# Expert phase of an mLSTM + two-MLP kernel: order of four engines written out by hand, six staging places for weights, a place for each slot's token weights

## The chip, the cores and the metric

One core of a Trainium2 chip runs the whole program. The metric is device time in microseconds (us) of one execution; lower is better. Times are medians of repeated runs on the chip; the profile is one further execution, recorded by the hardware profiler.

## What is computed

Three parts follow each other. An mLSTM recurrence (batch 4, 8 heads, 768 steps, head size 40) makes 3072 rows of 320 numbers. A dense MLP (320 to 2048 to 320, `h * sigmoid(h)` between) maps them. Then a top-1 mixture of eight experts follows, and this is the part that the change touches:

```python
logits = x @ w_gate                      # 3072 x 8
expert_idx = np.argmax(logits, axis=1)
...                                      # gate_w: the chosen expert's softmax weight
for e in range(8):
    xe = x[expert_idx == e]
    h = np.maximum(xe @ w1[e], 0.0)      # 320 -> 1024
    out[expert_idx == e] = gate_w[expert_idx == e, None] * (h @ w2[e])
```

## The kernel before

*Phase one* runs the recurrence in six chunks of 128 steps beside the dense MLP of the chunk before. While it runs, `rows(c)` routes each chunk: it finds each token's expert (`experts`), its row within the expert's list in DRAM (`place`), a power-of-two scale (`scale`), the gate weight (`weights`), and, in four `halves`, writes the token's 386-word row (value as a high and a low f16 half, gate weight, token number) to `rows_x` with an indirect store on GpSimd (POOL, line 931).

*Phase two* works through 28 *slots* of 128 tokens of one expert, listed in `line`: three early slots whose rows were fetched during phase one (`fetch_early`), 21 slots at offsets `kofi` that the last routing gives, and four late slots whose expert is known only at run time (`later_slots` computes it). A slot is

- `fetch`: SyncE (SP) reads the offset into a register, issues a transposing DMA of 128 rows into `xT` (line 1197) and a small DMA of gate weight and token number into `xm` (line 1199, pool of 5 buffers);
- `m_l1`: two halves of 32 matmuls of 128x128 (line 1212) into one of two PSUM buffers `ps_l1`; ScalarE (ACT) applies Relu and makes the high half `hh` (line 1217); VectorE (DVE) makes the low half `hl` (line 1218). A PSUM buffer is free when its `hl` is made;
- `m_l2`: 24 matmuls of 128x320 (lines 1231 to 1233); DVE scales into `ym` (line 1235, 2 buffers) and adds up the target row `sid` (line 1242, 3 buffers); POOL stores the 128 rows to the output (line 1243).

The experts' f32 weights come in 4 groups of 704 KB per expert (`load_w`: three or four DMAs on SP, lines 539 to 549) into one of two staging places of the pool `stg`. `go` makes the f16 high halves on ACT (lines 554, 555), its `tail` the low halves on DVE (lines 558, 562, 566), both into `w_all`; then the place is free. Experts 0 to 3 are loaded at fixed points of phase one (`at(p, ...)`, conversion 4 points later). The other 32 groups, experts 4 to 7 and four late experts, which take the room of experts 0 to 3, go through `weights_load` and `weights_split` in the slots' loop: on average 1.5 groups a slot, the next load of a place right after the conversion was recorded.

None of these lines fixes the order in which an engine gets its instructions. The framework's scheduler reorders them by dependences, priorities and a cost model of its own, engine by engine; each engine then runs its list strictly in order, and an instruction that waits holds back all behind it. The weights' conversions (ACT, DVE) and the slots' `hh`, `hl`, `ym`, `sid` share these lists, and the loads and fetches share SP's.

Of the kernel before, what the change touches and what calls it, by code (L numbers as in the profile page):

```python
# [33 lines left out]
def mlstm_moe_kernel(ctx, tc, q, k, v, ig, fg, og, w_in, w_out, w_gate, w1, w2, out):  # L34
# [127 lines left out]
    stg = ctx.enter_context(tc.tile_pool(name="stg", bufs=2))  # L162
# [369 lines left out]
    def load_w(k, g, e):  # L532

        cs = slice(g * GF, (g + 1) * GF)
        ts = stg.tile([128, WI], F32, tag="wi", name="e12")
# [6 lines left out]
        else:  # L542
            ee = bass.ds(e, 1)
            nc.sync.dma_start(out=t[:, 0:2, :], in_=w1[ee, 0:256, cs].rearrange("e (j p) f -> p (e j) f", p=128))
            for r in range(2):
                nc.sync.dma_start(
                    out=t[64 * r:64 * r + 64, 2, :], in_=w1[ee, 256:320, cs].rearrange("e p f -> p (e f)")
                )
# [24 lines left out]
    with contextlib.nullcontext():  # L573
# [446 lines left out]
        xme = const.tile([128, NE, 2], F32, name="xme")  # L1020
        done = const.tile([128, E], F32, name="done")

        def fetch_early():
            for i, (e, n) in enumerate(EARLY):
# [4 lines left out]
                xm[e, n] = xme[:, i, :]  # L1029
# [63 lines left out]
        for cf in todo:  # L1093
            l2(*cf)
        tails = []
        for i in range(2):
            rowt.append(th_v[i][:, 0:RW])
            nc.gpsimd.memset(rowt[-1][:, 352:384], 0.0)
        for fn in rows(NC - 1):
            t = fn()  # L1100
            while tails:
                tails.pop()()
            if callable(t):
                tails.append(t)
        tails.pop()()
# [4 lines left out]
        pn = ps_at.tile([128, E], F32, tag="at", name="ps_n")  # L1110
        nc.tensor.matmul(pn, ones, cum[:, NTT, :], start=True, stop=True)
# [7 lines left out]
        nc.vector.memset(zer, 0.0)  # L1119
        nc.vector.tensor_scalar(out=num, in0=pn, scalar1=-128.0, scalar2=None, op0=ALU.add)  # L1120

# [7 lines left out]
        nc.vector.tensor_tensor(out=kpos, in0=iota_k, in1=done.unsqueeze(2).to_broadcast(sk), op=ALU.add)  # L1129
        nc.vector.tensor_tensor(out=kfit, in0=kpos, in1=num.unsqueeze(2).to_broadcast(sk), op=ALU.min)  # L1130
        nc.vector.tensor_tensor(out=kofi, in0=kfit, in1=ebase.unsqueeze(2).to_broadcast(sk), op=ALU.add)
        nc.vector.tensor_tensor(out=kpos, in0=kpos, in1=kfit, op=ALU.subtract)
        nc.vector.tensor_scalar(out=kneg, in0=kpos, scalar1=iota_p, scalar2=NONE, op0=ALU.is_gt, op1=ALU.mult)
# [56 lines left out]
        hT = {}  # L1190

        def fetch(i, row):
# [8 lines left out]
        def m_l1(i, k):  # L1201
            x = xT.pop(i)
            hh = mp.tile([128, NF2, 128], F16, tag="hh", name="hh")
            hl = mp.tile([128, NF2, 128], F16, tag="hl", name="hl")
            hT[i] = (hh, hl)
            for r in range(2):
                ps = ps_l1.tile([128, 4, 128], F32, tag="l1", name="ps_m1")
                for jj in range(4):
                    f = 4 * r + jj
                    terms = [(0, 0), (1, 1), (2, 2), (3, 0), (4, 1), (0, 3), (1, 4), (2, 5)]  # L1210
                    for n, (a, m) in enumerate(terms):
# [43 lines left out]
        def later(i):  # L1255
            return ((E + i, 0), i % ND, ofi[0:1, i:i + 1], neg[:, i:i + 1])
# [89 lines left out]
```

## Time and profile before

| | us |
|---|---|
| median of 3 runs | 814.64 (805.28 to 817.34) |
| the profiled execution's own time | 814.33 |
| its span in the profile | 812.2 |
| TensorE (PE) busy in the span | 689.3 |
| mean granted TensorE clock, 1.0 = full | 0.925 |

A row of the timeline view reads: start, length, engine, source line, operation, output <- inputs, count, and in brackets how long the engine had sat idle and what released it. SPq is SyncE's queue, where the length is that of issuing the DMA. A row of the waits view reads: who <- for whom: us in total, times, longest. A row of the windows view gives the busy time of each engine in a stretch, and at its end granted clock, share of the 16 DMA engines, and GB/s moved.

### The profile page before, as it was taken

What the parts mean: (1) busy time and instruction counts of PE and PEld (TensorE: products, weight loads), DVE (VectorE), ACT (ScalarE), POOL (GpSimd) and SP (SyncE); (2) the same over time, 40 slices, a digit from 0 to 9 for tenths busy, and PEclk for the clock granted to TensorE, in tenths of its full rate; (3) what the DMA queues carried; (4) which work ended last, traced back from release to release, by engine and by line L of the source; (5) the groups of instructions that cost most, each with busy time, mean ns of one, the idle gap of its engine ahead of it and who ended that gap; (6) DMA issues with size and microseconds to landing.
All of it is one profiled execution on the core that took longest, in us unless ns stands there. A gap on an engine that the chain in (4) does not pass through costs nothing. (4 is left out here: it accounts for less than half of the span.)

```text
span 812.2 us, 15662 instructions
## 1 busy us (share of the span) xinstructions
PE 689.3 (85%) x5840; PEld 490.0 (60%) x5840; DVE 513.3 (63%) x1262; ACT 375.8 (46%) x816; POOL 98.6 (12%) x134
## 2 busy tenths in 40 slices
PE   4866999998888999889998977996685978878994
PEld 3724766765555556556665634555575867767883
DVE  6686689888778856676777566457555355544231
ACT  5563467766566545556654354435233233332110
POOL 3010001112001211020011001101100000111110
PEclk9677799999899999999999998997979998999997
DMA  8757898997889565453441243224675555565210
GB/s 156 145 133 190 199 175 211 211 177 170 167 170 175 117 124 102 89 118 79 93 88 52 72 130 104 50 67 135 143 177 137 100 155 142 144 145 122 52 25 22
DMA packets 243309, 102.83 MB, mean 127 GB/s; under 512 B 181621, under 2 KB 237112, under 8 KB 243224
## 3 DMA queue, kind: packets, MB, share of 16 engines
q1 hardware_dynamic: 239860, 92.99, 53.9%
q0 software_dynamic: 2880, 8.68, 2.9%
q8 instruction: 48, 0.79, 0.4%
q14 instruction: 37, 0.30, 0.1%
q10 hardware_dynamic: 484, 0.08, 0.1%
HBM read 71.64 MB, written 11.59 MB: 102 GB/s over the span
## 5 line engine op out<-in xcount | busy, mean ns | idle before, releaser
L961 PE MATMUL ps_h<-w_all 128*128 128x512 f16 x768 | 194.6, 393 | 10.8 <-ACT w_all L466 5.5
L1212 PEld LDWEIGHTS <-w_all 128*128 128x128 f16 x1792 | 116.7, 106 | 42.0 <-issue 40.2
L1212 PE MATMUL ps_m<-xT,w_all 128*128 128x128 f16 x1600 | 106.5, 233 | 35.0 <-DVE hl L1218 35.0
L961 PEld LDWEIGHTS <-w_all 128*128 128x128 f16 x768 | 74.7, 101 | 87.9 <-issue 15.2
L1005 PE MATMUL ps_y<-w_all 128*128 128x328 f16 x332 | 102.2, 308 | 7.3 <-ACT w_all L1013 6.7
L554 ACT ACTIVATE w_all<-e 128x768 f16<-128x768 f32 x48 | 40.4, 842 | 134.1 <-DMA e<-in_moe_w_dram 124.1
L1007 PE MATMUL ps_y<-w_all 128*128 128x328 f16 x332 | 101.8, 307 | 0.3 <-DVE w_all L988 0.3
L1006 PE MATMUL ps_y<-w_all 128*128 128x328 f16 x332 | 101.9, 307 | 0.0
L988 DVE SCALAR_TENSOR_TENSOR w_all<-w_all 128x512 f16<-128x512 f32 x83 | 57.2, 689 | 39.3 <-ACT w_all L985 38.4
L558 DVE SCALAR_TENSOR_TENSOR w_all<-e,w_all 128x512 f16<-128x512 f32 x48 | 33.1, 689 | 75.4 <-ACT w_all L554 72.7
L985 ACT ACTIVATE w_all<-w_all 128x512 f16<-128x512 f32 x83 | 51.9, 625 | 56.9 <-DVE w_all L980 56.5
L241 ACT ACTIVATE w_all<-w_all,bias_t 128x128 f32<-128x128 f32 x160 | 52.9, 391 | 41.8 <-POOL w_all L207 41.7
L1231 PE MATMUL ps_m<-w_all,hh 128*128 128x320 f16 x224 | 67.2, 300 | 5.8 <-ACT hh L1217 5.8
L1232 PE MATMUL ps_m<-w_all,hh 128*128 128x320 f16 x224 | 67.3, 301 | 0.0
L1233 PE MATMUL ps_m<-w_all,hl 128*128 128x320 f16 x224 | 67.3, 300 | 0.0
L980 DVE SCALAR_TENSOR_TENSOR w_all<-w_all,ps_h 128x512 f32<-128x512 f32 x83 | 56.5, 681 | 14.2 <-ACT w_all L977 14.0
L1217 ACT ACTIVATE hh<-ps_m 128x512 f16<-128x512 f32 x56 | 32.3, 590 | 68.8 <-PE ps_m L1212 65.6
L977 ACT ACTIVATE w_all<-ps_h 128x512 f32<-128x512 f32 x83 | 48.5, 585 | 23.7 <-PE ps_h L961 22.0
L1218 DVE SCALAR_TENSOR_TENSOR hl<-ps_m,hh 128x512 f16<-128x512 f32 x56 | 38.3, 685 | 27.6 <-ACT hh L1217 27.5
L318 PEld LDWEIGHTS ps_pv<-w_all 128*128 128x128 f32 x384 | 50.6, 207 | 7.0 <-issue 2.7
L318 PE MATMUL ps_pv<-w_all 128*128 128x41 f32 x384 | 50.4, 293 | 3.6 <-issue 2.0
L1243 POOL DMA_INDIRECT out_dram<-ym,sid x28 | 27.8, 992 | 206.6 <-DVE ym L1235 187.5
(210 smaller groups left out, 1123.1 us busy)
## 6 DMA issues: line engine op xcount, KB each, us to landing
e<-in_moe_w_dram SPq DMA_DIRECT2D x48, 320.0 KB
e<-in_moe_w_dram SPq DMA_DIRECT2D x48, 256.0 KB
w_all<-lam_d SPq DMA_DIRECT2D x20, 512.0 KB
w_all<-in_moe_w_out_dram SPq DMA_DIRECT2D x16, 320.0 KB
wi<-in_moe_w_in_dram SPq DMA_DIRECT2D x8, 512.0 KB
e<-in_moe_w_dram SPq DMA_DIRECT2D x32, 128.0 KB
w_all<-in_k_dram SPq DMA_DIRECT2D x24, 160.0 KB
w_all<-in_q_dram SPq DMA_DIRECT2D x24, 160.0 KB
```

Source lines behind the costliest of these rows:

```text
L241: nc.scalar.activation(out=lt[:, h, :], in_=lt[:, h, :], func=AF.Exp, bias=bias_t[:, c, b * H + h:b * H + h + 1])
L318: nc.tensor.matmul(pv[:, h, :], u["lam"][:, h, :], u["v"][:, h, :], start=True, stop=True)
L961: nc.tensor.matmul(ps, a, x, start=(i == 0), stop=(i == len(terms) - 1))
L980: nc.vector.scalar_tensor_tensor(out=th, in0=th, scalar=1.0, in1=ps, op0=ALU.add, op1=ALU.mult)
L988: nc.vector.scalar_tensor_tensor(out=gl, in0=th, scalar=SG, in1=gh, op0=ALU.mult, op1=ALU.subtract)
L1005: nc.tensor.matmul(ps, gh[:, ts], woh[:, f, :], start=(f == 0), stop=False)
L1006: nc.tensor.matmul(ps, gh[:, ts], wol[:, f, :], start=False, stop=False)
L1007: nc.tensor.matmul(ps, gl[:, ts], woh[:, f, :], start=False, stop=(f == NF - 1))
L1212: nc.tensor.matmul(ps[:, jj, :], w1c[k][:, a, f * 128:f * 128 + 128], x[:, m, :], start=(n == 0), stop=(n == len(terms) - 1),)
L1231: nc.tensor.matmul(ps, hh[:, f, :], w[:, 0, :], start=(f == 0), stop=False)
L1232: nc.tensor.matmul(ps, hh[:, f, :], w[:, 1, :], start=False, stop=False)
L1233: nc.tensor.matmul(ps, hl[:, f, :], w[:, 0, :], start=False, stop=(f == NF2 - 1))
```

## The change

1. From the last two `l2` calls of phase one to the last slot, everything stands inside `tc.manual_schedule` for PE, ACT, DVE and SP: these four get their instructions in the order of the source. POOL stays with the scheduler.
2. The source is rewritten as a pipeline: `m_l1` is split into `m_half`; the last `rows(NC - 1)` is dealt out between the halves of slots 0 and 1; a slot `i` is: fetch of slot `i + 2`, half 0, low halves of one weight group and the next load into its place, `hl`, half 1, `hl`, one conversion (on odd slots from 7 one more of each), then the second layer of slot `i - 1`.
3. Staging has six places: `stg` has 3 buffers, and from slot 5 on three more (`more`) lie in the room of expert 0, whose slots are over. The late experts therefore use the rooms of experts 1 to 4.
4. `xm` gets a place for each of the 28 slots (`xms`); `xT` rotates over the four buffers `Qs`, `Ks`; `ym` has 4 buffers, `sid` 6.
5. In phase one, the conversion stands 8 (experts 0, 1) or 7 points after the load instead of 4. A run-time expert's third weight part is one DMA instead of two.

```diff
-    stg = ctx.enter_context(tc.tile_pool(name="stg", bufs=2))
+    stg = ctx.enter_context(tc.tile_pool(name="stg", bufs=3))
...
-            at(p + 4, lambda: w_go.pop(0)())
+            at(p + (8 if i < 2 * NG else 7), lambda: w_go.pop(0)())
...
+        xT_b = turns([x[:, 0:6, :] for x in Ks[1:] + Qs + Ks[:1]])
...
-            xT[i] = mp.tile([128, 6, 128], F16, tag="xT", name="xT")
+            xT[i] = next(xT_b)
             nc.sync.dma_start_transpose(out=xT[i], in_=r.bitcast(F16)[:, 0:768])
-            xm[i] = mp.tile([128, 2], F32, tag="xm", name="xm", bufs=5)
+            if i in place_of:
+                xm[i] = xms[:, place_of[i], :]
...
-            y = mp.tile([128, DM], F32, tag="ym", name="ym", bufs=2)
+            y = mp.tile([128, DM], F32, tag="ym", name="ym", bufs=4)
...
-            sid = mp.tile([128, 1], I32, tag="sid", name="sid")
+            sid = mp.tile([128, 1], I32, tag="sid", name="sid", bufs=6)
...
+        more = [F32V[:, i * WI:(i + 1) * WI] for i in range(WN // (2 * WI))]
...
+        def split():
+
+            if w_go:
+                go, place = w_go.pop(0)
+                w_low.append((go(), place))
+
+        def low_and_load():
+
+            if w_low:
+                t, place = w_low.pop(0)
+                t()
+                load(place)
...
+        with tc.manual_schedule(engines={ENG.PE, ENG.Activation, ENG.DVE, ENG.SP}):
+
+            for cf in todo:
+                l2(*cf)
...
+            for i in range(NE, NE + 2):
+                get(i)
+            for i in range(2, len(line)):
+                if i > 2:
+                    get(i + 2)
+                t = half(i, 0)
+                low_and_load()
+                t()
+                if i > 5 and i % 2:
+                    split()
+                t = half(i, 1)
+                t()
+                if i > 5 and i % 2:
+                    low_and_load()
+                if i == 3:
+                    later_slots()
+                split()
+                if i == 5:
+                    for x in more:
+                        load(x)
+                second(i - 1)
+            second(len(line) - 1)
```

ACT at the seam of the phases, before: L1013 evicts the dense MLP's last results (`ps_y`), L554 and L555 convert a weight group (`e_...` is its staging place), L1217 is a slot's Relu.

```order
L554 ACTIVATE w_all<-e_6020 128x3x256
L555 ACTIVATE w_all<-e_6020 128x2x320
L1013 ACTIVATE w_all<-ps_y_5234 128x328
L1013 ACTIVATE w_all<-ps_y_5238 128x328
L1013 ACTIVATE w_all<-ps_y_5242 128x328
L1013 ACTIVATE w_all<-ps_y_5246 128x328
L554 ACTIVATE w_all<-e_6061 128x3x256
L555 ACTIVATE w_all<-e_6061 128x2x320
L1217 ACTIVATE hh<-ps_m_5867 128x512
```

The same place of the changed kernel; its L1011, L1208 and L858 are the L1013, L1217 and L860 of before (L858 is an exponential of the routing).

```order
L1011 ACTIVATE w_all<-ps_y_5234 128x328
L1011 ACTIVATE w_all<-ps_y_5238 128x328
L1011 ACTIVATE w_all<-ps_y_5242 128x328
L1011 ACTIVATE w_all<-ps_y_5246 128x328
L1208 ACTIVATE hh<-ps_m_5796 128x512
L858 ACTIVATE le<-ld 128x32
L1208 ACTIVATE hh<-ps_m_5845 128x512
```

The two conversions ahead of and behind the evictions are gone from here: the first conversion of phase two now stands behind both Relus of slot 2.

SP in the middle of phase two, before: the fetch of a slot (L1197, L1199) and the load of a weight group (L544 to L549).

```order
L1197 DMA_TRANSPOSE xT<-rows_x 128x6x128
L1199 ISA
L1199 DMA xm<-rows_x 128x2
L544 ISA
L544 DMA e_7155<-in_moe_w_dram 128x2x256
L546 ISA
L546 DMA e_7155<-in_moe_w_dram 64x256
L546 ISA
L546 DMA e_7155<-in_moe_w_dram 64x256
L549 ISA
L549 DMA e_7155<-in_moe_w_dram 128x2x320
```

After, slots 7 and 8: two loads (L540 to L542) and the fetch for slot 10 with its register load (L1180 to L1188).

```order
L540 DMA e_6758<-in_moe_w_dram 128x2x256
L541 DMA e_6758<-in_moe_w_dram 128x1x256
L542 DMA e_6758<-in_moe_w_dram 128x2x320
L540 DMA e_6803<-in_moe_w_dram 128x2x256
L541 DMA e_6803<-in_moe_w_dram 128x1x256
L542 DMA e_6803<-in_moe_w_dram 128x2x320
L1180 TENSOR_LOAD kofi
L1180 ISA x2
L1183 ISA
L1183 DMA_TRANSPOSE Ks_109<-rows_x 128x6x128
L1188 ISA
L1188 DMA xms<-rows_x 128x2
```

The `xm` DMA, behind which each load stood before, now writes a place that nothing else uses; what remains ahead of a load is the fetch two slots ahead and the conversion that frees the load's own place.

## Rows read from the trace of the kernel before

**Rows 1.** The page's head.
```profile
span 812.2 us, 15662 instructions
```

**Rows 2.** Windows view of stretches of phase two.
```profile
core 0: us, PE busy (x) PEld busy (x) DVE busy (x) ACT busy (x) POOL busy (x), PEclk, DMA share, GB/s
547.50:800.20 252.70, 209.56 (x2469) 180.34 (x2466) 118.06 (x264) 77.46 (x123) 30.79 (x31) 0.92 0.50 121
580.00:740.00 160.00, 127.06 (x1433) 109.65 (x1431) 76.81 (x139) 54.37 (x83) 16.45 (x17) 0.90 0.61 147
590.00:600.00 10.00, 9.04 (x88) 7.96 (x88) 5.63 (x12) 3.89 (x6) 0.97 (x1) 0.78 0.90 192
656.00:663.00 7.00, 5.26 (x66) 4.34 (x63) 3.16 (x6) 1.47 (x2) 0.11 (x1) 1.00 0.84 229
```

**Rows 3.** Timeline of PE, one slot without a wait and the next with one.
```profile
576.28 3.74 PE L1212 MATMUL ps_m<-xT,w_all 128*128 128x128 f16 x64
579.86 0.30 PE L1231 MATMUL ps_m<-w_all,hh 128*128 128x320 f16 x1
...
582.98 0.30 PE L1233 MATMUL ps_m<-w_all,hl 128*128 128x320 f16 x1
590.15 5.78 PE L1212 MATMUL ps_m<-xT,w_all 128*128 128x128 f16 x64 [6.87 <-DVE hl L1218]
595.76 0.30 PE L1231 MATMUL ps_m<-w_all,hh 128*128 128x320 f16 x1
```

**Rows 4.** Waits from 560 us on, and SP's own from 540 us on (SPq).
```profile
ACT w_all L554 <- DMA e<-in_moe_w_dram: 87.3, 25, 9.0
PE ps_m L1212 <- DVE hl L1218: 35.0, 13, 6.9
DVE sid L1242 <- DMA out_dram<-ym,sid: 28.6, 15, 3.6
SPq L1199 <- DVE ym L1235: 53.0, 18, 5.4
```

**Rows 5.** Timeline of all engines, one turn of the loop in the middle of phase two.
```profile
644.17 0.54 DVE L1235 TENSOR_SCALAR ym<-ps_m,xm 128x320 f32<-128x320 f32 x1
644.75 0.35 SPq L1199 DMA_DIRECT2D xm<-rows_x  x1
645.35 0.37 SPq L544 DMA_DIRECT2D e<-in_moe_w_dram  x1
650.55 0.84 ACT L554 ACTIVATE w_all<-e 128x768 f16<-128x768 f32 x1 [5.53 <-DMA e<-in_moe_w_dram]
...
653.34 0.55 DVE L1235 TENSOR_SCALAR ym<-ps_m,xm 128x320 f32<-128x320 f32 x1
```

**Rows 6.** Timelines of PE, ACT, POOL and SP at the seam of the phases.
```profile
547.53 3.74 PE L1212 MATMUL ps_m<-Qs,w_all 128*128 128x128 f16 x64
557.09 0.45 PE L1231 MATMUL ps_m<-w_all,hh 128*128 128x320 f16 x1 [5.83 <-ACT hh L1217]
...
550.74 0.84 ACT L554 ACTIVATE w_all<-e 128x768 f16<-128x768 f32 x1 [5.40 <-DMA e<-in_moe_w_dram]
552.20 1.43 ACT L1013 ACTIVATE w_all<-ps_y 128x328 f32<-128x328 f32 x4
...
568.22 0.98 POOL L931 DMA_INDIRECT rows_x<-w_all,di  x1 [0.30 <-issue]
...
571.07 1.28 SPq L1197 DMA_TRANSPOSE xT<-rows_x  x1
```

**Rows 7.** Waits of ACT and PE in phase one, 150 to 547 us.
```profile
ACT w_all L554 <- DMA e<-in_moe_w_dram: 30.0, 13, 4.5
PE ps_y L1005 <- ACT w_all L1013: 6.7, 3, 4.2
```

**Rows 8.** What the stores to the output (tile sid) show: the last one, and issue to landing.
```profile
802.61 0.97 POOL L1243 DMA_INDIRECT out_dram<-ym,sid  x1 [3.90 <-DMA out_dram<-ym,sid]
...
DMA to landing us min/median/max: 2.5/3.5/5.3
```

More of the change, by code (lines that the diff above doesn't have):

```diff
@@ L1187, in mlstm_moe_kernel @@
         ofi = rt.tile([128, NSLOT], I32, name="ofi")
-        hT = {}
+        hT, place_of = {}, {}
+        xT_b = turns([x[:, 0:6, :] for x in Ks[1:] + Qs + Ks[:1]])
         def fetch(i, row):
@@ new lines, in m_half @@
+        def m_half(i, k, r):
+            if r == 0:
+                hh = mp.tile([128, NF2, 128], F16, tag="hh", name="hh", bufs=2)
+                hl = mp.tile([128, NF2, 128], F16, tag="hl", name="hl", bufs=2)
+                hT[i] = (hh, hl)
+            hh, hl = hT[i]
+            x = xT[i]
+            ps = ps_l1.tile([128, 4, 128], F32, tag="l1", name="ps_m1")
+            for jj in range(4):
+                f = 4 * r + jj
+                terms = [(0, 0), (1, 1), (2, 2), (3, 0), (4, 1), (0, 3), (1, 4), (2, 5)]
+                for n, (a, m) in enumerate(terms):
+                    nc.tensor.matmul(
+                        ps[:, jj, :], w1c[k][:, a, f * 128:f * 128 + 128], x[:, m, :],
+                        start=(n == 0), stop=(n == len(terms) - 1),
+                    )
+            fs = slice(4 * r, 4 * r + 4)
+            nc.scalar.activation(out=hh[:, fs, :], in_=ps, func=AF.Relu)
+            return lambda: nc.vector.scalar_tensor_tensor(
+                out=hl[:, fs, :], in0=ps, scalar=0.0, in1=hh[:, fs, :], op0=ALU.max, op1=ALU.subtract
+            )
@@ L1255, in later, with load @@
         def later(i):
-            return ((E + i, 0), i % ND, ofi[0:1, i:i + 1], neg[:, i:i + 1])
+            return ((E + i, 0), 1 + i % ND, ofi[0:1, i:i + 1], neg[:, i:i + 1])
         line += [later(i) for i in range(ND)]
+        place_of.update({x[0]: i for i, x in enumerate(line)})
         w_load = [(e, g) for e in [*range(4, E), *range(E, E + ND)] for g in range(NG)]
-        w_go, w_tail, ex = [], [], {}
-        def weights_load():
+        w_go, w_low, ex = [], [], {}
+        more = [F32V[:, i * WI:(i + 1) * WI] for i in range(WN // (2 * WI))]
+        def load(place):
             if w_load:
@@ L1305, in mlstm_moe_kernel, with get, second @@
-        m_l2(line[-1][0], line[-1][1], line[-1][3])
+                go, place = w_go.pop(0)
[5 more added lines that the diff above has]
+                load(place)
+        def get(i):
+            if NE <= i < len(line):
+                fetch(line[i][0], line[i][2])
+        def second(i):
+            m_l2(line[i][0], line[i][1], line[i][3])
+        for _ in range(3):
+            load(None)
@@ new lines, in mlstm_moe_kernel @@
+        ENG = mybir.EngineType
+        with tc.manual_schedule(engines={ENG.PE, ENG.Activation, ENG.DVE, ENG.SP}):
+            for cf in todo:
+                l2(*cf)
+            for i in range(2):
+                rowt.append(th_v[i][:, 0:RW])
+                nc.gpsimd.memset(rowt[-1][:, 352:384], 0.0)
+            experts, place, scale, weights, *halves = rows(NC - 1)
+            half = lambda i, r: m_half(line[i][0], line[i][1], r)
+            t = half(0, 0)
+            experts()
+            t()
+            t = half(0, 1)
+            place()
+            scale()
+            weights()
+            t()
+            h = [x() for x in halves[0:2]]
+            t = half(1, 0)
+            h.pop(0)()
+            t()
+            h += [x() for x in halves[2:]]
+            h.pop(0)()
+            t = half(1, 1)
+            h.pop(0)()
+            h.pop(0)()
+            count()
+            t()
+            second(0)
+            for i in range(NE, NE + 2):
[5 more added lines that the diff above has]
+                low_and_load()
+                t()
+                if i > 5 and i % 2:
+                    split()
+                t = half(i, 1)
+                t()
+                if i > 5 and i % 2:
[8 more added lines that the diff above has]
+            second(len(line) - 1)
@@ L1313, in mlstm_moe_kernel @@
                     now(load_w(k, g, e))
-                m_l1(name, k)
+                for r in range(2):
+                    m_half(name, k, r)()
                 m_l2(name, k, no)
```

102 lines of the change are left out of this document (21 added, 81 removed).

## The prediction, made before the changed kernel ran

> **What bounds the kernel now.** I read the windows first, to see where TensorE (PE) isn't full. Phase two, from the first expert matmul to the last, takes 252.7 us of the 812.2 us span, and PE is busy for 209.6 of them, at a mean granted clock of 0.92 [rows 1, 2]. The timeline of PE then gives the price of a slot that waits for nothing [rows 3]: its 64 matmuls of 128x128 take 579.86 - 576.28 = 3.58 us, and its 24 of 128x320 stand (582.98 - 579.86) / 23 = 0.1357 us apart, 3.26 us together. So a slot costs 6.84 us, and 28 of them 191.5 us. Phase two is 252.7 - 191.5 = 61.2 us longer than its matmuls need. That is the most which a better order can give back here, unless phase one changes too.
>
> The waits say where it goes [rows 4]. PE waited 13 times, 35.0 us in all, for a low half `hl`, which frees a PSUM buffer. At the seam it waited 5.83 us once more, for `hh` [rows 6]. After such a stop the next 64 matmuls are slow as well: 5.61 us instead of 3.58 in the slot at 590.15 [rows 3], where the granted clock of the ten microseconds around it is 0.78 [rows 2], so part of them ran at the lower level of 1.2 GHz. Some ten stops at 2 us each are the remaining 20 us of the 61.2.
>
> Why is `hl` late? ACT waited 87.3 us for weights to land, in front of conversions, and Relus stand behind these in its list. SP waited 53.0 us to issue an `xm` DMA until a `ym` was made, with weight loads behind that. DVE waited 28.6 us in `sid` for stores to land [rows 4]. One turn shows that this is a closed ring [rows 5]: `ym` at 644.17 frees an `xm` buffer, SP issues the load behind it at 645.35, the weights land at 650.55, ACT converts, Relu and `hl` follow, PE goes on, and the next `ym` comes at 653.34. The ring turns once in 9.17 us, where PE needs 6.84. Transfers run at 147 GB/s meanwhile, at a share of 0.61 [rows 2]: the DMA engines are not full, they are asked too late.
>
> **The change part by part.**
>
> *Places for `xm`, `ym`, `sid`.* The 53.0 and 28.6 us have no cause left: every `xm` writes a place of its own, and `sid` is made behind its own `ym` with six buffers. The ring is cut at SP. Nothing is late in its place on DVE or ACT: they were busy 118.1 and 77.5 us in phase two [rows 2], which is 61% and 40% of the 193 us that remain.
>
> *Six staging places.* A load is now issued about four slots, some 25 us, before its conversion stands in ACT's list; the load of [rows 5] took 650.55 - 645.35 = 5.2 us. ACT's 87.3 us go as long as the DMA engines keep up. Per slot they must move 1.5 groups of 0.721 MB, 0.197 MB of rows and a store of 0.164 MB: 1.44 MB in 6.84 us, 211 GB/s. The fullest longer stretch of phase two shows 229 GB/s at a share of 0.84 [rows 2]. So it fits, with 8% to spare. It is tightest after slot 5, where four groups are issued at once: 3.24 MB need 14.2 us at that rate, 7.3 more than the slot has. If transfers are served in the order of their issue, the fetch for slot 8 queues behind what is left, and it has about 12 us; with the 5.2 us in which the fetch at 571.07 was there for 576.28 at the latest [rows 3, 6], it may be a microsecond or two late. From both sides: nothing, if 229 GB/s isn't the ceiling; at 192 GB/s, the other full stretch [rows 2], a slot takes 1.44 / 0.192 = 7.5 us, 0.67 more for the 15 slots in which loads run, plus some 4 us at the burst, 14 us. I take 2, nearer the better row, which holds two loads and a fetch together, as phase two will.
>
> A rule of the Trainium skill speaks against this part. [rows 2] shows what was moved with at most two groups under way. The page "DMA: Bandwidth & Descriptors", section "Queues, rings and completion order", says that all that SP issues shares one ring per DMA engine, and that a ring's descriptors are consumed in order. By it a fetch really waits for every group issued before it, and 192 GB/s would cost the 14 us above; without it the fetch would overtake and cost nothing. No wait of PE for a fetch stands in the trace of before, so no run here shows it yet.
>
> *The seam.* Before, ACT stood until 550.74 for weights in front of the last evictions, which began at 552.20 although PE had finished phase one's matmuls at about 547.5 [rows 6]. Now evictions and Relus come first, so the routing starts 4.7 us earlier. PE's order is slots 0 and 1 with the routing's small matmuls between, then the second layer of 0, slot 2, the second layer of 1, then slot 3: 3 x 3.58 + 2 x 3.26 = 17.3 us of work. One stop is new: half 1 of slot 1 needs the PSUM buffer that `hl` of slot 0 frees, behind routing work on DVE. It is bounded by nothing and by the 5.83 us that PE waited at this seam before [rows 6]; I take 1, nearer nothing, since ACT no longer holds it back. Slot 3 needs the last routed rows. In the trace, evictions to the fetch of slot 3 took 571.07 - 552.20 = 18.9 us [rows 6], and at most 5.2 more until it was there: 24.1 us after 547.5 at worst, against 18.3 us of PE work. The wait is 0 to 5.8 us. I take 2, since that chain held other waits for weights, now gone, but its four indirect stores in a row stay.
>
> *Order within a slot.* `low_and_load` stands ahead of `hl` on DVE, and a conversion ahead of the second Relu on odd slots. The `hl` of half 0 is wanted when the next slot begins, 6.84 - 1.79 = 5 us after its matmuls; DVE and ACT had 118.1 / 28 = 4.2 and 77.5 / 28 = 2.8 us of work a slot [rows 2], the stretch with two conversions included. I count nothing. If a conversion's load is late, what is left of the 5 us is its cover, and beyond it PE stops.
>
> *Phase one.* ACT waited 30.0 us for weights there, of which PE felt at most the 6.7 us behind late evictions [rows 7]. A later conversion and a third place take away some; five conversions of phase two no longer stand there, but those of phase one stand closer together. Between a gain of 7 and a loss of 4 I take a gain of 1.
>
> *The DMA less for run-time experts* saves SP issue time that nothing waits for: nothing.
>
> The sum: phase two takes 191.5 + 1 + 2 + 2 = 196.5 us instead of 252.7, a gain of 56.2, with phase one 57.2. The tail behind the last matmul stays. The profiled execution took 814.33 us, the median of the runs is 814.64, the same within a tenth of a per cent. 814.3 - 57.2 = 757.1: I predict 757 us.
>
> **The rivals.**
>
> *The transfers become the bound.* For it: 8% to spare is little, the share already was 0.90 in a stretch that moved 192 GB/s [rows 2], and a deep queue lets fetches come late every second slot. Against it: 229 GB/s was reached. At 192 GB/s the 14 us make it 769. At 180, a slot takes 8.0 us, 1.17 more for 15 slots, plus 6 at the burst: 23.5 us, 779.
>
> *The DMA engines give no more than the mean of now.* If 147 GB/s [rows 2] were what this mix of transfers can get, a slot would take 9.8 us while loads run, 3 more for 15 slots, and some 8 at the burst: 53 us, so 808, no change that can be told. Against it stand all the stretches above 190.
>
> *Stores in series make it slower.* Each store to the output waits until the one before it has landed: the last one shows 3.90 us of idle time for that [rows 8]. Four `ym` buffers don't shorten a series; if loads queued deeply made stores land late, the series would set the pace. They land 2.5 to 5.3 us after issue [rows 8]. Phase two now takes 252.7 / 28 = 9.0 us a slot. From about 9.6 us a slot, landing some 8.6 us after an issue of 1 us [rows 8], the kernel is slower by over 2%; at 10 us to land, 28 x 11 = 308 us, 55 more than now, 870. It needs more than one and a half times the longest time seen, in every slot.
>
> **How the numbers follow.** The forecast with its small waits, 747 to 766, has 0.65; transfers as the bound, 766 to 798, 0.26; the mean of now 0.06; stores in series 0.03. The range goes from 747 (no wait but the 1 us, and 7 from phase one: 814.3 - 60.2 - 7) to 782 (about 178 GB/s). A change of 2% is 16 us, what a measurement of this kernel can tell from none: faster is 0.91, same 0.06, slower 0.03.
>
> **What would show it.** Right: phase two from first to last expert matmul in 194 to 200 us, PE busy almost throughout at a granted clock near 1.0, slots 6.84 us apart, no `xm` wait on SP, ACT's wait for weights under 20 us, GB/s above 200 from slot 6 to 21. Wrong: PE waits for `xT` every second slot with a share near 1 (first rival); a wait for `hl` behind ACT's conversions that stays; PE stops in slots 3 and 8 of over 6 us each; a phase one that ends more than 7 us earlier or later than 547.5.

## The result, and the profile after

The changed kernel takes 775.45 us, median of 4 runs (771.19 to 777.74), against 814.83 us (805.28 to 817.34, 4 runs) for the kernel before: a ratio of 0.953, 95% interval 0.946 to 0.961. The forecast was 757 us with a range of 747 to 782. The direction and the range held; the central figure was 18 us too low. 775.45 us lies in the band that the forecast gave to its first rival, the transfers as the bound (766 to 798).

The profiled execution took 771.19 us, its span is 769.5 us. Three stretches make up its difference to the profiled execution of before (814.33 us):

| stretch | before | after | gain | forecast |
|---|---|---|---|---|
| phase one, to the first expert matmul | 547.53 | 538.15 | 9.4 | 1 |
| phase two, to the end of the last expert matmul | 252.6 | 218.9 | 33.7 | 56.2 |
| behind it, to the end of the span | 12.1 | 12.5 | -0.4 | 0 |
| outside the span | 2.1 | 1.7 | 0.4 | 0 |

So phase two lost some 22 us against the plan, and phase one gave 8.4 us back that were not planned. The windows of after answer to [rows 2] (columns as there):

```profile
core 0: us, PE busy (x) PEld busy (x) DVE busy (x) ACT busy (x) POOL busy (x), PEclk, DMA share, GB/s
538.10:757.20 219.10, 197.58 (x2469) 169.34 (x2467) 126.23 (x281) 78.49 (x127) 35.09 (x31) 0.97 0.76 141
574.00:600.00 26.00, 19.58 (x248) 16.59 (x245) 14.92 (x27) 8.90 (x14) 4.54 (x4) 0.93 0.81 169
600.00:720.00 120.00, 108.06 (x1331) 92.86 (x1332) 67.79 (x122) 46.99 (x74) 16.66 (x14) 0.96 1.02 183
```

PE's time in phase two fell from 209.56 to 197.58 us busy, at a clock of 0.97 where it was 0.92. What matters is the last row: from 600 to 720 us the DMA share is 1.02, yet only 183 GB/s are moved. [rows 2] had 229 GB/s at a share of 0.84. The waits, from 540 to 770 us, answer to [rows 4]:

```profile
engine line waited for: us in total, times, longest us
ACT hh L1208 <- PE ps_m L1203: 120.0, 42, 12.7
PE ps_m L1203 <- DMA Qs<-rows_x: 11.7, 4, 7.9
PE ps_m L1203 <- DMA Ks<-rows_x: 6.7, 3, 3.1
PE ps_m L1203 <- DVE hl L1209: 1.8, 3, 0.9
PE ps_m L1203 <- issue: 0.7, 1, 0.7
PE ps_r L877 <- DVE cum L870: 0.5, 1, 0.5
```

Of the four large waits of [rows 4], three are gone: ACT no longer waits for weights (87.3 us), nor SP for a `ym` (53.0), nor DVE for a store (28.6). PE's 35.0 us for low halves are now 1.8. In their place stand 18.4 us for fetched rows (`Qs` and `Ks` are the buffers they land in), in 7 stops: at slot 8, and at every second slot from 12 to 22. All of PE's stops together are 21.4 us, and its busy time is 6.1 us over the 191.5 that the matmuls need at full clock: 191.5 + 21.4 + 6.1 = 219.0, all of phase two. The longest stop shows both parts in the timeline of SP and PE (start, duration, instruction, in brackets the idle time before it and what ended that):

```profile
573.41 0.41 SPq L542 DMA_DIRECT2D e<-in_moe_w_dram  x1
574.81 1.27 SPq L1183 DMA_TRANSPOSE Ks<-rows_x  x1
...
577.91 2.36 SPq L542 DMA_DIRECT2D e<-in_moe_w_dram  x1
...
581.42 2.15 SPq L542 DMA_DIRECT2D w_all<-in_moe_w_dram  x1
...
585.07 3.50 SPq L542 DMA_DIRECT2D w_all<-in_moe_w_dram  x1
...
586.58 3.74 PE L1203 MATMUL ps_m<-Ks,w_all 128*128 128x128 f16 x64
...
590.18 3.08 SPq L542 DMA_DIRECT2D w_all<-in_moe_w_dram  x1
...
594.20 1.88 SPq L1183 DMA_TRANSPOSE Qs<-rows_x  x1
...
601.45 6.06 PE L1203 MATMUL ps_m<-Qs,w_all 128*128 128x128 f16 x64 [7.87 <-DMA Qs<-rows_x]
```

Slot 8 stands still for 7.87 us, and its 64 matmuls then take 6.06 us instead of slot 7's 3.74. The fetch for slot 7 was issued at 574.81. Behind it come the four groups of slot 5, and SP spends 2.15 to 3.50 us on issuing each group's last DMA, where one took 0.41 at 573.41. The fetch for slot 8 goes out at 594.20, when slot 8 is already due (586.58 + 6.84 = 593.4).

### The profile page after: what moved, and what is told of

Its sections match the earlier page's. It is cut to its first block, busy times and chain, and to the rows that moved or that the text cites. A ratio compares the mean times of both kernels' runs of the same rounds, so it can differ in the third digit from the quotient of the medians.

```text
span 769.5 us, 15581 instructions
## 1 busy us (share of the span) xinstructions
PE 674.0 (88%) x5840; PEld 477.4 (62%) x5840; DVE 516.6 (67%) x1262; ACT 374.5 (49%) x816; POOL 102.5 (13%) x134
## 4 chain that ended last, share of the span: by engine, by line
PE 42%; DMA 22%; DVE 15%; ACT 8%; issue 6%; SPq 3%; POOL 2%; POOLq 0%; ACTq 0%; DVEq 0%
PE ps_h L959 11%; PE ps_m L1203 9%; DMA w_all<-lam_d 5%; DMA Qs<-rows_x 4%; DMA out_dram<-ym,sid 3%; PE ps_y L1000 3%; DMA e<-in_moe_w_dram 3%; PE ps_pv L318 3%; ACT w_all L241 2%; DMA w_all<-Qs 2%; PE ps_y L1003 2%; DVE w_all L978 2%; PE ps_y L1004 2%; PE ps_y L1005 2%; POOL w_all L207 2%
## 5 line engine op out<-in xcount | busy, mean ns | idle before, releaser
L959 PE MATMUL ps_h<-w_all 128*128 128x512 f16 x768 | 197.1, 398 | 5.5 <-ACT w_all L466 3.5
L959 PEld LDWEIGHTS <-w_all 128*128 128x128 f16 x768 | 75.2, 102 | 84.0 <-issue 15.2
L1203 PEld LDWEIGHTS <-w_all 128*128 128x128 f16 x1792 | 105.8, 100 | 25.2 <-DMA Qs<-rows_x 13.0
L1003 PE MATMUL ps_y<-w_all 128*128 128x328 f16 x332 | 101.0, 304 | 2.0 <-ACT w_all L1011 2.0
L1004 PE MATMUL ps_y<-w_all 128*128 128x328 f16 x332 | 100.7, 303 | 0.0
L1005 PE MATMUL ps_y<-w_all 128*128 128x328 f16 x332 | 100.6, 303 | 0.0
L1208 ACT ACTIVATE hh<-ps_m 128x512 f16<-128x512 f32 x56 | 33.3, 595 | 132.6 <-PE ps_m L1203 120.0
L1203 PE MATMUL ps_m<-Qs,w_all 128*128 128x128 f16 x896 | 54.8, 224 | 13.5 <-DMA Qs<-rows_x 11.7
L1203 PE MATMUL ps_m<-Ks,w_all 128*128 128x128 f16 x896 | 54.1, 222 | 7.4 <-DMA Ks<-rows_x 6.7
L207 POOL TENSOR_SCALAR_AFFINE_SELECT w_all<-w_all 128x1024 f32<-128x1024 f32 x20 | 24.4, 1219 | 233.7 <-DMA w_all<-lam_d 146.2
L1234 POOL DMA_INDIRECT out_dram<-ym,sid x28 | 32.0, 1141 | 176.3 <-DVE sid L1233 128.5
```

Of the source, the lines that this page charges most:

```text
L959: nc.tensor.matmul(ps, a, x, start=(i == 0), stop=(i == len(terms) - 1))
L1003: nc.tensor.matmul(ps, gh[:, ts], woh[:, f, :], start=(f == 0), stop=False)
L1004: nc.tensor.matmul(ps, gh[:, ts], wol[:, f, :], start=False, stop=False)
L1005: nc.tensor.matmul(ps, gl[:, ts], woh[:, f, :], start=False, stop=(f == NF - 1))
L1203: nc.tensor.matmul(ps[:, jj, :], w1c[k][:, a, f * 128:f * 128 + 128], x[:, m, :], start=(n == 0), stop=(n == len(terms) - 1),)
```

## The experiments

Three theories stood at the start. **A**: the DMA engines are full, so less work for them, or the same work better spread, is what helps. **B**: a fetch is late because it stands behind loads in SP's list and queue. **C**: the burst of slot 5 alone is at fault. Later questions were what made the gain, the places or the order by hand, and whether phase one's 9.4 us are real. Lengths of phase two below are read from PE's timeline of each profile, as in the table above.

| kernel | median us (runs) | ratio to before, 95% | first expert matmul, us | phase two, us |
|---|---|---|---|---|
| after | 775.45 (4) | 0.953, 0.946 to 0.961 | 538.15 | 218.9 |
| after, again | 771.93 (4) | 0.957, 0.947 to 0.967 | 537.68 | 218.9 |
| e1, plain fetch | 764.89 (4) | | 535.41 | 211.2 |
| e2, burst spread | 770.33 (4) | 0.957, 0.948 to 0.967 | 531.82 | 220.9 |
| e3, loads by ACT | 773.53 (4) | 0.963, 0.952 to 0.973 | 532.71 | 225.4 |
| e4, three places | 762.53 (4) | 0.946, 0.933 to 0.960 | 531.90 | 214.8 |
| i4, three places, rows 3 ahead | 763.36 (4) | 0.938, 0.934 to 0.942 | 543.38 | 209.4 |
| i2, loads spread | 753.31 (6) | 0.933, 0.923 to 0.942 | 539.12 | 204.1 |
| i3, loads spread, rows 3 ahead | 752.86 (4) | 0.925, 0.921 to 0.930 | 541.49 | 199.8 |
| e5, scheduler's order | 813.07 (4) | 0.998, 0.993 to 1.003 | 546.81 | 253.4 |
| e8, order by hand on ACT alone | 813.45 (10) | 1.005, 1.001 to 1.009 | 544.25 | 259.5 |
| e6, before with places | 806.38 (4) | 0.992, 0.987 to 0.996 | 553.11 | 243.1 |
| e7, before with phase one's edits | 803.15 (10) | 0.993, 0.988 to 0.998 | 544.52 | 251.3 |

The kernel before had medians of 809.86 us beside e1 to e4, 814.4 beside e5, e6, i3 and i4, and 810.3 beside after again, i2, e7 and e8. These three groups ran on three different chips, so totals, and the ends of phase one, are best compared within a group. e1 has no ratio, since it leaves the transposition out.

**The kernel after, again.** No edit.

> The kernel after, unchanged, for a second profile: how far the end of phase one (538.15 us in the first profile, 547.53 in the kernel before) and the length of phase two (218.9 us) scatter. If phase two is set by its transfers: 216 to 222 us again. If phase one's 9.4 us are real: it ends at 535 to 541; if they are scatter: anywhere from 531 to 550. Time 768 to 779.

Phase two is 218.9 us in both profiles, to the tenth, with 17.5 us of waits for rows (18.4 before). So a few microseconds of difference in phase two mean something, as far as two profiles can tell. Phase one ends at 537.68, in the range given for a real gain, but its end is less firm, see below.

**e1, a plain fetch.**

```diff
-            nc.sync.dma_start_transpose(out=xT[i], in_=r.bitcast(F16)[:, 0:768])
+            nc.sync.dma_start(out=xT[i], in_=r.bitcast(F16)[:, 0:768].rearrange("p (j q) -> p j q", j=6))
```

> The kernel after with its 25 later fetches as plain DMAs of the same rows and bytes; their transposition is left out. Theory A (the DMA engines are full: between 600 and 720 us the profile of after shows a share of 1.02 at 183 GB/s, and a transposing fetch takes about 1.45 us of all of them): a plain fetch of 0.197 MB should take about 0.9, 0.6 less in each of some 15 slots, so PE's 18.4 us of waits for rows fall by about half and the time is 764 to 769. Theory B (a fetch is late because it stands behind weight loads in SP's list and in the ring, whatever the engines have to spare): the waits stay, 773 to 778.

The four runs lie apart (756.64, 760.75 and twice 769.03; median 764.89): all are under B's 773, and two are even under A's 764. Phase two is 7.7 us shorter, and PE's waits for rows are 10.5 us instead of 18.4, about half, as A asked. The DMA view from 600 to 720 us (queue, kind: packets, MB, share of the 16 engines; then what was issued) gives more than was asked. After:

```profile
q1 hardware_dynamic: 30111, 19.56, 94.3%
...
Qs<-rows_x SPq DMA_TRANSPOSE x8
Ks<-rows_x SPq DMA_TRANSPOSE x8
```

With the plain fetch:

```profile
q1 hardware_dynamic: 19811, 19.22, 55.4%
...
Ks<-rows_x SPq DMA_DIRECT2D x10, 192.0 KB
Qs<-rows_x SPq DMA_DIRECT2D x8, 192.0 KB
```

Nearly the same bytes in the same time, with two fetches more, need a share of 55.4% and not 94.3%. It is the transposition that fills the engines. But B isn't dead: the stop at slot 8 is still 5.78 us long here, though the engines have room. The windows and SP's timeline of this kernel:

```profile
580.00:590.00 10.00, 10.00 (x112) 7.97 (x109) 6.21 (x11) 5.71 (x9) 1.04 (x1) 1.00 0.61 189
```

```profile
576.23 3.14 SPq L542 DMA_DIRECT2D w_all<-in_moe_w_dram  x1
...
581.01 3.06 SPq L542 DMA_DIRECT2D w_all<-in_moe_w_dram  x1
...
589.28 0.36 SPq L1183 DMA_DIRECT2D Qs<-rows_x  x1
```

At a share of 0.61 each third DMA of the burst still holds SP for some 3 us, and the fetch waits in SP's list until 589.28. So the burst's stop has a cause of its own, SP held while it issues, beside the full engines of the steady part. What holds SP there no run shows. Of the 18.4 us of waits, 7.9 went with the transposition. The 10.5 that are left, 5.8 at slot 8 and 4.7 at four later slots, come with room on the engines, as B says. A part of the 7.9 may be B's too, since SP issues a plain fetch in mostly 0.36 us and took 1.26 to 2.60 for a transposing one.

**e2, the burst spread.**

```diff
-                if i == 5:
-                    for x in more:
-                        load(x)
+                if 5 <= i < 5 + len(more):
+                    load(more[i - 5])
```

> The kernel after with the three loads into expert 0's old place issued one each in slots 5, 6 and 7 and not together in slot 5. Theory C (the burst alone is the fault: SP is held by full queues, and slot 8's rows come 7.9 us late): that wait goes, nothing takes its place, 767 to 769. Theory A (full engines): the same bytes must be moved by slot 21, the 7.9 us come back as more and smaller waits in slots 8 to 21, 772 to 777. Theory B: in between, 769 to 773, since fewer loads stand ahead of each fetch.

The 7.9 us stop went, the longest is now 5.2, but the sum of PE's waits for rows stayed: 11.3 + 6.9 = 18.2 us, and phase two is 220.9. C falls as an explanation of the total: with full engines the delay comes back in other slots. The median of 770.33 is in B's range; in the profile it is phase one, at 531.82, that is shorter than in after, not phase two.

**e3, loads issued by ACT.** As e2, and:

```diff
-                w_go.append((load_w(k, g, e, place), place))
+                w_go.append((load_w(k, g, e, place, nc.scalar), place))
```

> As e2_spread, and all weight loads of phase two are issued by ACT, so that SP issues fetches alone and a fetch stands behind no load in SP's list or in its queue. Theory B (order): no wait of PE for rows is left, 757 to 762. Theory A (full engines): a fetch shares the engines with the loads and what PE no longer waits for rows it waits for low halves behind late weights on ACT; share still near 1 from 600 to 720 us, 768 to 778. ACT's own issues, some 0.4 us each where no queue is full, cost nothing by either, unless full queues hold ACT in front of a Relu: then slower than 778.

773.53 us. From the waits of PE and ACT, 530 to 770 us:

```profile
ACT hh L1209 <- issue: 26.5, 7, 5.9
...
PE ps_m L1204 <- DVE hl L1210: 23.2, 19, 3.6
```

Not one wait for rows is left, and nothing is gained: 23.2 us for low halves took the place of 18.2 us for rows. ACT now waits for its weights and for its own issues in front of Relus: it spends 64 us of phase two on issuing the 87 DMAs of the loads, and the 26.5 us above stand in front of Relus. B is right that no wait for rows is left. That its time of 757 to 762 was missed doesn't decide against it, since the edit puts this new work on the engine whose Relus PE needs; the time is in A's range, but full engines and ACT's issues can't be told apart here. Since loads and fetches have queues of their own in this kernel, its DMA view from 600 to 720 us prices them apart:

```profile
q10 hardware_dynamic: 14925, 15.96, 52.8%
q1 hardware_dynamic: 13714, 2.90, 38.4%
q0 software_dynamic: 672, 2.08, 6.8%
...
out_dram<-ym,sid POOLq DMA_INDIRECT x15, 6.2
...
Qs<-rows_x SPq DMA_TRANSPOSE x8
Ks<-rows_x SPq DMA_TRANSPOSE x7
```

q10 carries the loads, q1 the fetches, q0 the stores. 15 fetches take 0.384 x 120 = 46.1 us of all 16 engines, 3.07 each, for 0.19 MB. Loads take 63.4 us for 15.96 MB, so a group of 0.721 MB takes 2.86. Stores take 8.2 us, 0.54 each. A slot with 1.5 groups therefore needs 4.3 + 3.1 + 0.5 = 7.9 us of the engines, and PE needs 6.84. In the kernel after, the fetches of SP from 600 to 720 us, 15 of them from 601.06 to 712.70, stand 8.0 us apart. That is A, with its price. It is the price in a stretch that is already full: the shares add up to 0.98, so their sum by slot gives that stretch's own pace, and what is new in it is how the time is divided.

With no loads beside it a fetch is cheaper. The last six of the kernel before, from 740 to 780 us, take 0.209 x 40 / 6 = 1.4 us each, near the 1.45 that e1's expectation took:

```profile
q1 hardware_dynamic: 5664, 1.19, 20.9%
...
xT<-rows_x SPq DMA_TRANSPOSE x6
```

The traces' records of single packets show where the rest goes. A fetch is 768 packets of 256 bytes, and half of them last 18 ns or less in either kernel. But in after, from 600 to 720 us, most fetches have some 18 packets that stay open for up to 4.4 us and end at one instant. Counting packets of over 0.6 us, there are 15 such holds; they cover 44 of the 120 us, and transfers start at 70 GB/s inside them and 249 outside. In the kernel before they cover 8 us of the same stretch. So most of the price is time in which the engines stand in a fetch and move little. What ends a hold, no run shows.

**e4, three staging places.**

```diff
-                if i == 5:
-                    for x in more:
-                        load(x)
```

> The kernel after with three staging places in phase two and not six: the loads into expert 0's old place are left away, no burst, and a load is issued about two slots ahead of its conversion. If six places are what brings the gain: ACT waits for weights again, 785 to 800. Theory A: the engines are as full, the waits move from rows to weights, 773 to 783. Theory C (the burst is the fault): 765 to 769.

762.53 us (three runs from 759.78 to 765.04, one at 775.47), below all three expectations; phase two is 214.8 us, 4.1 shorter than with six places. Waits of PE and ACT:

```profile
ACT w_all L552 <- DMA e<-in_moe_w_dram: 74.3, 23, 5.0
...
PE ps_m L1203 <- DMA Ks<-rows_x: 7.2, 3, 4.0
PE ps_m L1203 <- DMA Qs<-rows_x: 4.6, 3, 2.7
PE ps_m L1203 <- DVE hl L1209: 3.8, 7, 0.9
```

ACT waits 74.3 us for weights again, nearly the 87.3 of [rows 4], and PE hardly feels it: 3.8 us. So ACT's wait was not the loss; where its conversions stand decides that. The three places in expert 0's old area did not bring the gain, and fewer loads ahead of each fetch even spare PE 6.6 us of waits for rows. By total time the two kernels can't be told apart (the intervals overlap).

**i4, three places and rows three slots ahead** (`get(i + 3)`, as in i3 below).

> As e4_three_places, with rows fetched three slots ahead and not two. Theory A: ACT bears the wait for late weights (74.3 us in e4_three_places, none of which PE felt), and PE's 11.8 us of waits for rows go: 752 to 760. If three slots ahead only puts a fetch behind the same loads: 760 to 766. If rows ahead of weights make conversions so late that PE waits for low halves: over 766.

763.36 us, in the range of the second expectation, but not by its mechanism: waits for rows are gone, as A asked, and those for low halves rose from 3.8 to 14.1 us, as the third feared. Phase two is 5.4 us shorter than e4's in the profile; that the medians don't differ says little, since the two ran on different chips and i4's phase one ended 11.5 us later.

**i2 and i3, the loads spread.** Phase two leaves the engines idle at both ends: in after the share is 0.38 from 540 to 574 us and 0.26 from 720 to 760. The edit loads three groups more at the seam, and draws the conversions out.

```diff
+        first = [F32V[:, 3 * WN + i * WI:3 * WN + (i + 1) * WI] for i in range(len(more))]
...
             second(0)
+            for x in first:
+                load(x)
...
-                if i > 5 and i % 2:
+                if i > 2 and i % 3 == 0:
...
-                if i == 5:
-                    for x in more:
-                        load(x)
```

A place of `first` is followed by one of `more` once it is free. i3 also fetches with `get(i + 3)`.

> The kernel after with the engines' work spread: three more groups are loaded at the seam into expert 6's place (free until its own weights come), each then goes over to a place of expert 0's old area in its turn, so there is no burst; a second conversion comes every third slot from slot 3, not every second from slot 7, and rows are fetched three slots ahead. Theory A (full engines between 574 and 720 us, idle before and behind): PE's waits for rows shrink to under 6 us, 757 to 764. If fetch and load only change places in the queue: 768 to 778.

> As i3_first_even_3ahead, with rows fetched two slots ahead as in the kernel after. Theory A (it is the spread of the transfers that counts): 751 to 758, PE's waits for rows under 8 us. If the third slot ahead carries the gain: 760 to 768, with 10 us or more of waits for rows left.

752.86 us for i3, 4 us better than A's range, and 753.31 for i2, inside A's; i2 ran beside the second run of after (771.93) and no run of the one comes near one of the other (749.36 to 756.54 against 769.87 to 775.29). These beat both kernels. i3's windows:

```profile
541.50:741.30 199.80, 194.34 (x2469) 167.47 (x2466) 125.57 (x280) 78.65 (x127) 33.49 (x31) 0.99 0.86 155
...
600.00:660.00 60.00, 60.00 (x784) 52.21 (x782) 38.81 (x71) 25.20 (x41) 10.38 (x9) 1.00 1.08 181
660.00:720.00 60.00, 60.00 (x774) 51.95 (x771) 38.61 (x71) 26.36 (x42) 9.40 (x9) 1.00 1.00 168
```

The engines are as full from 600 to 720 us as in after, and move no more, but PE is busy for all 120 us, because fewer loads are due there: 20 groups are issued beside 18 fetches, where after issues 23 beside 16. By e3's prices i3's transfers need 57 + 55 + 10 = 122 us of the engines in these 120. PE waits 3.9 us for low halves and 0.4 for rows in the whole of phase two, which takes 199.8 us. With rows two ahead (i2) it is 3.8 and 3.9 us, and 204.1: the spread, of loads and conversions together, carries the gain, and the third slot ahead some 4 us more of phase two.

**e5, the scheduler's order.**

```diff
-        with tc.manual_schedule(engines={ENG.PE, ENG.Activation, ENG.DVE, ENG.SP}):
+        with contextlib.nullcontext():
```

> The kernel after with all its edits, but the block in which the order is written by hand is opened without the manual schedule, so that the scheduler orders the engines' lists as it did before. Theory P (places make the gain: xm, ym and sid cut the ring, staging feeds ACT): as after, 770 to 780. Theory O (the order by hand makes it): the scheduler puts weight conversions in front of Relus and the seam's evictions again, 790 to 806.

813.07 us: with every place of the change in it, nothing is gained. That is slower than theory O gave. Its waits are those of [rows 4] once more: ACT for weights in front of conversions (37.1 and 30.0 us), PE 35.7 for low halves, DVE 31.3 in `sid`. ACT, DVE and PE in its timeline:

```profile
640.40 1.95 PE L1203 MATMUL ps_m<-Qs,w_all 128*128 128x128 f16 x32 [2.39 <-DVE hl L1209]
641.24 0.84 ACT L552 ACTIVATE w_all<-w_all 128x768 f16<-128x768 f32 x1 [2.35 <-DMA w_all<-in_moe_w_dram]
...
642.88 0.74 ACT L553 ACTIVATE w_all<-w_all 128x640 f16<-128x640 f32 x1 [0.80 <-DMA w_all<-in_moe_w_dram]
...
646.59 0.84 ACT L552 ACTIVATE w_all<-w_all 128x768 f16<-128x768 f32 x1 [2.97 <-DMA w_all<-in_moe_w_dram]
647.34 1.07 ACT L1208 ACTIVATE hh<-ps_m 128x512 f16<-128x512 f32 x2
...
648.07 0.68 DVE L1209 SCALAR_TENSOR_TENSOR hl<-ps_m,hh 128x512 f16<-128x512 f32 x1
648.81 1.39 PE L1203 MATMUL ps_m<-Qs,w_all 128*128 128x128 f16 x22 [3.20 <-DVE hl L1209]
```

The half begun at 640.40 was ready at 642.35. Its Relu comes at 647.34, because two conversions stand in front of it on ACT, and the second waits 2.97 us for weights that are still on the way; `hl` follows, and PE stops for that. Six places don't help a list that asks for a group as soon as it is on its way.

**e8, the order by hand on ACT alone.**

```diff
-        with tc.manual_schedule(engines={ENG.PE, ENG.Activation, ENG.DVE, ENG.SP}):
+        with tc.manual_schedule(engines={ENG.Activation}):
```

> The kernel after with the order by hand for ACT's list alone; PE's, DVE's and SP's lists are the scheduler's. Theory R (e5_scheduler is slow because conversions whose weights have not landed stand in front of Relus on ACT): ACT's wait for weights falls under 20 us and the time is 770 to 785. Theory L (the four lists work only together: DVE's list puts low halves and sid in front of what PE needs, SP's list puts fetches behind loads): 795 to 812.

813.45 us; theory R falls, and L's range is missed by 1.5 us. ACT waits only 4.5 us for weights, as R asked, and DVE has taken its part:

```profile
DVE sid L1233 <- DMA xms<-rows_x: 74.7, 13, 19.9
...
PE ps_m L1203 <- DVE hl L1209: 35.4, 13, 5.6
...
PE ps_m L1203 <- DMA xms<-rows_x: 15.2, 1, 15.2
```

The scheduler's list for DVE puts `sid` of a slot where it waits for that slot's fetch, with low halves behind it, and PE itself stops once for 15.2 us. A list in order is only as good as those that it waits for. Which of DVE's and SP's lists would have to be written by hand besides ACT's was not tried.

**e6 and e7, parts of the change on the kernel before.** e6 gives `xm`, `ym` and `sid` their places, e7 has three staging places and phase one's later conversions. Both put fetched rows into the buffers of q and k, for room, so their gains don't add.

```diff
-            xm[i] = mp.tile([128, 2], F32, tag="xm", name="xm", bufs=5)
+            if i in place_of:
+                xm[i] = xms[:, place_of[i], :]
...
-            y = mp.tile([128, DM], F32, tag="ym", name="ym", bufs=2)
+            y = mp.tile([128, DM], F32, tag="ym", name="ym", bufs=4)
```

> The kernel before with places of its own for each xm, four ym, six sid (and the rows fetched into the buffers of q and k, which makes the room for them); two staging places, the scheduler's order and phase one stay. Theory P, ring cut at SP: SP's 53.0 us and DVE's 28.6 us of waits go, a load is issued as soon as its staging place is free, phase two falls by 15 to 25 us, 785 to 797. Theory S (two staging places are a ring of their own: load 5.2 us, conversion, low half, next load): ACT's wait for weights stays, 802 to 812.

```diff
-            at(p + 4, lambda: w_go.pop(0)())
+            at(p + (8 if i < 2 * NG else 7), lambda: w_go.pop(0)())
...
-    stg = ctx.enter_context(tc.tile_pool(name="stg", bufs=2))
+    stg = ctx.enter_context(tc.tile_pool(name="stg", bufs=3))
```

> The kernel before with the edits that bear on phase one alone: three staging places and the later conversions of the first four experts (and the rows of phase two fetched into the buffers of q and k, which makes the room). Theory G (they give phase one's 9.4 us): the time falls by 7 to 11 us, 802 to 808, and phase one ends at 535 to 541. Theory N (scatter of the profiles): 809 to 817, phase one ends at 543 to 553.

e6 gains 0.8%, in S's range. SP's wait for a `ym` is gone, as theory P said, but ACT's wait for weights and PE's for low halves stay, as S said; in its profile phase two is 9.5 us shorter than in before, where P had 15 to 25, and phase one 5.6 longer:

```profile
ACT w_all L554 <- DMA e<-in_moe_w_dram: 78.8, 28, 8.7
PE ps_m L1216 <- DVE hl L1222: 34.4, 20, 7.7
```

e7 gains 0.7%, 5.4 us of 810.3 with an interval from 1.5 to 9.4. The time is in G's range, but phase one's end in its profile, 544.52, is in N's, 3 us earlier than in before; the profiled execution, 810.35 us, was one of its slower ones (median 803.15). So the edits gain, and where the 5.4 us lie is not settled.

## Why the prediction was right or wrong

**The ring.** That the waits of SP, DVE and ACT would go, and low halves with them, was right (87.3, 53.0, 28.6 and 35.0 us became 0, 0, 0 and 1.8). The reason given, that places cut the ring at SP, was wrong in its weight: places alone bring 0.8% (e6), and places without the order nothing (e5). It is the order by hand that puts conversions and `sid` behind what PE waits for. The order with the places of before was not tried, so what it brings alone is open.

**Transfers, the step that failed.** "So it fits, with 8% to spare" counted bytes: 1.44 MB in 6.84 us against 229 GB/s. By that a fetch costs 0.197 / 0.229 = 0.9 us. e3 shows 3.07 beside loads, as much as a whole group of weights, since it is transposed on its way (e1 takes that out, and the share falls from 94.3% to 55.4%). The kernel before did not show this: its fetches without loads beside them took 1.4 us, and with that the sum would still have fitted, an estimate, with e3's prices for loads and stores, of 4.3 + 1.4 + 0.5 = 6.2 us a slot. What the step had wrong is to count bytes, whatever the kind of transfer and whatever runs beside it. With 3.07 us for a fetch a slot needs 7.9 us of the engines, the first rival's case, and close to its "at 180 GB/s, 8.0". The 4 us taken for transfers, burst and slot 3's fetch were 18.4 us of waits, and most of 6.1 us of slower matmuls behind them. About 8 of the 18.4 went with the transposition (e1); the rest stayed with room on the engines, which fits SP's issue in order. What the forecast's remark "to 782 (about 178 GB/s)" covered is where the kernel ended, since 183 GB/s were moved.

**The burst.** "A microsecond or two late" was 7.87 us. The mechanism was right, a fetch behind four groups; that SP spends up to 3.5 us on issuing one DMA was not in the sum. The rule cited from the Trainium skill (page "DMA: Bandwidth & Descriptors", section "Queues, rings and completion order") has a fetch wait behind the groups issued before it. The runs fit it: in e1, with room on the engines, slot 8 still stops for 5.78 us, and in e3, with the fetches in a queue of their own, no wait for rows is left. But much of slot 8's delay arises before the ring, in SP's list, which issues the fetch only at 594.20 (in e1 at 589.28); the two were not told apart. What the wait alone costs e3 doesn't tell, since its 773.53 us hold ACT's issues as well.

**A second figure of the page.** Its section "Latency and other measured facts" gives a transposing DMA 261 GB/s, or more where the source is contiguous. No run here agrees: e3's fetches moved 2.90 MB in 46.1 us of the engines' time, 63 GB/s, while loads got 15.96 / 63.4 us = 252 GB/s. The six fetches without loads beside them come to 1.19 MB in 8.4 us, 142 GB/s. The measurement decides here.

**The seam.** 3 us were counted for it. The profile of after shows stops of 0.60 and 0.85 us for low halves and 0.5 for `cum`, and slot 3, begun at 558.73, waits for nothing. The sum was 1 us too dear, by two errors that partly offset each other: the new stops cost 1.95 us where 1 was taken, and the last routed rows cost none of their 2.

**Order within a slot.** Counted at nothing, and right: 1.8 us of waits for low halves in all, the seam's 1.45 included.

**Phase one.** A gain of 1 us was taken, with 7 as its bound; the two profiles of after show 9.4 and 9.9. One part is likely real: e7 gains 5.4 us with the edits alone, though not shown to be in phase one. Another is scatter: the nine profiles of kernels whose phase one is the same as after's and whose seam is ordered by hand on all four engines reach the first expert matmul between 531.82 and 543.38 us, 537 on average. Most of that lies between chips (531.8 to 535.4, 537.7 to 539.1 and 541.5 to 543.4 us on the three), and it goes with the granted clock: up to 530 us its mean is 0.96 in the two profiles at 531.82 and 532.71, and 0.93 in the one at 543.38. The profile of before, with 547.53, had 0.93 too, the first one of after 0.95. So a part of the 9.4 us probably is clock; why the clock differed, no run shows. The bound of 7 came from PE's waits for late evictions alone, in one execution. What else shortens phase one wasn't tried.

**Stores in series.** Excluded rightly: in phase two after, POOL waited for a store to land once, 4.0 us, behind the last slot.

So 757 became 775: 22.4 us more in phase two (218.9 where 196.5 stood), 8.4 less from phase one give the 771.2 of the profiled execution, which lay 4.3 under the median. That the time stayed well inside the range is in part luck: with phase one where the forecast had it, the profiled execution would have taken 779.6. By the forecast's own signs its mechanism failed: phase two is not at 194 to 200 us, 183 GB/s were moved from 600 to 720 us where over 200 were named, PE waits for rows at every second slot with a share near 1, slot 8 stops for over 6 us, and phase one ended more than 7 us early. The signs that held are those of SP, ACT and the low halves.

## What to carry to other kernels

Price each kind of DMA in engine time and add those times per turn of the loop; bytes over the best GB/s of a mixed stretch hide a transposing fetch that costs as much as nearly four times its bytes. Take the price from a stretch as full as the one to be forecast: the same fetch took 1.4 us without loads beside it and 3.07 among them. When the DMA engines are full in the middle of a phase and idle at its ends, moving loads to the ends is worth more than a longer queue in the middle (i2: 19 us less than after beside it, with the same transfers, while e4's shorter queue lost nothing). More buffers do nothing for a list in order that asks for each buffer as soon as it is filled: look first at what stands in front of the instruction that the busiest engine waits for.

## What the runs showed of the hardware

A DMA that transposes 128 rows of 1.5 KB took 3.07 us of all 16 engines' time next to weight loads, and 1.4 without them. In the full stretch some 18 of its packets stay open for up to 4.4 us and end together, and transfers start at 70 GB/s meanwhile. A plain one is estimated at 0.7 (e1's 66.5 us for 21 groups and 18 fetches, shared out by bytes). The DMA share can thus stand at 1 with 168 to 183 GB/s, and at 0.61 with 189.

SP's issue of a DMA took 0.41 us in a quiet stretch and up to 3.50 us behind three or four groups, and up to 3.14 where the share was 0.61. SP's list stands still meanwhile, so a burst delays everything behind it on SP, before any queue does.

Phase one of one and the same code ended up to 11.6 us apart in profiles of kernels that differ only behind it, and at most 3.6 us apart on one chip; its end went with the granted clock, from 531.82 us at a mean of 0.96 to 543.38 at 0.93. A few microseconds in one stretch of one profile are therefore no finding where the stretch wasn't changed; phase two of the same kernel agreed to 0.1 us.
